# Attention with a softmax off by one and a gated long convolution: products of the shared keys with the values in tiles of 64 by 64

## The chip, the core and the metric

The kernel runs on one core of a Trainium2 chip, in one launch. The metric is the time of that launch on the device in microseconds (us). TensorE does the matrix products, VectorE (DVE), ScalarE (ACT) and GpSimd (POOL) do what is elementwise, SyncE (SP) issues most transfers.

## The reference, cut to what matters

```python
batch, n_heads, seq, head_dim = (8, 12, 448, 64)

def _attn_ref(q, k, v):
    scale = 1.0 / np.sqrt(q.shape[-1])
    scores = scale * np.matmul(q, k.transpose(0, 1, 3, 2))
    m = np.max(scores, axis=-1, keepdims=True)
    e = np.exp(scores - m)
    attn = e / (np.sum(e, axis=-1, keepdims=True) + np.exp(-m) + 1e-09)
    return np.matmul(attn, v).astype(np.float32)

def _moe_ref(x, w_proj, filter_fft, w_out):
    B, S, D = x.shape
    proj = x @ w_proj
    x1, x2, x3 = (proj[..., :D].copy(), proj[..., D:2 * D].copy(), proj[..., 2 * D:].copy())
    X2 = np.fft.rfft(x2, n=S, axis=1)
    H = np.fft.rfft(filter_fft, n=S, axis=0)[None, :, :]
    x2_conv = np.fft.irfft(X2 * H, n=S, axis=1)
    y = x1 * x2_conv * x3
    return (y @ w_out).astype(np.float32)
```

The output of attention, its heads side by side, is the `x` of the second function.

## The kernel before, in words

**Attention works on pairs of heads.** Eight batch elements of twelve heads make 48 pairs; `attention(i)` does pair `i`. A head has 448 keys: three tiles of 128 and a rest of 64. The rests of both heads of a pair share one tile (t = 0): rows 0 to 63 belong to head u = 0, rows 64 to 127 to head u = 1. These are the shared keys.

**Scores.** For the key tiles t = 1, 2, 3 `scores(t)` (L844) makes the transposed scores, keys on the partitions and queries along the free side, in quarters of the array: a head has 64 channels, so the two heads take the two halves of its rows, and the 128 keys of a tile are cut in two halves of 64 columns. Four matmuls (u and d) make one tile for both heads. The shared tile (L846) is one matmul of the full array. ScalarE takes the exponent (`exps`, L857 for t = 1, 2, 3 and L863 for the shared tile) into the bfloat16 tiles `e` and `er`.

**Value products.** Here the exponents are the stationary operand and the values (64 columns and a column of ones that gives the sum of the row, 65 in all) the moving one. Queries go in four tiles n of 128, the last of them padded. `out_rests` (L875) does the shared keys of both heads: for each n and each head u a matmul with 64 rows of `er` and 128 query columns, into the PSUM bank of that head. `out_rest(u)` (L883) adds the three full key tiles, twelve matmuls of the full array for each head. `norm` then divides on VectorE (L896 to L898).

**Where `out_rests` stands.** The program is written by a planner (`Plan`): every task names its engine, what it needs, makes, takes and gives, and a fixed list, `ORDER`, says in which order the tasks of each engine stand. Nothing is reordered at run time. `out_rests` of pair j is no task of its own in most cases; it is emitted at the end of a score task of the next pair, right behind the matmuls of L844:

```python
host = (2 if b == 0 or i % 2 == 0 else 3) if i and i != NHP else None
...
ex = with_rests(i - 1) if t == host else dict(cost=0.0, emit=lambda: None, ...)
```

Only at pairs 5 and 47 it is a task by itself. So 46 of the 48 stand behind L844.

**The second part.** `dense(b)` makes the three projections (L1072, L1094, L1194), the convolution by a short Fourier transform as matmuls (L1144, L1148, L1240), the gate on VectorE (L1209, L1284), and the output product (L1008), copied to SBUF by L1316 and sent out. Its tasks stand on TensorE between those of attention.

**Inputs.** q, k and v come in by transfers that SP issues; POOL casts them to bfloat16; from the third batch element on (`loaded`) the transposed keys and queries, `kT` and `qT`, are made by transposing transfers (L610, L603), and the output of attention is transposed in the same way into `xT` (L971).

Of the kernel before, what the change touches and what calls it, by code (L numbers as in the profile page):

```python
# [301 lines left out]
def kernel(  # L302
# [11 lines left out]
    nc = tc.nc  # L314
# [57 lines left out]
    vn = [const.tile([128, NHP, 7, DH + 1], BF16, name=f"vn{i}") for i in range(2)]  # L372
# [457 lines left out]
    def attention(i):  # L830
        b, hp = divmod(i, NHP)
        P = T.setdefault(i, {})
# [32 lines left out]
        def out_banks():  # L865
            return pair(("op", i))[:, :, 0 : NST * (DH + 1)].rearrange("p u (n d) -> p u n d", n=NST)

        def out_bank(u):
            return out_banks()[:, u]

        def out_rests():
            for n in range(NST):
                for u in range(2):
                    c = slice(64 * u, 64 * u + 64)
                    nc.tensor.matmul(  # L875
                        out_bank(u)[:, n, :], P["e"][0][c, n * 128 : n * 128 + 128], vn[b % 2][c, hp, 3, :],
                        start=(n == 0), stop=False,
                    )

        def out_rest(u):  # L880
            for n in range(NST):
# [65 lines left out]
        if i in (NHP - 1, n_batches * NHP - 1):  # L947
            ex = with_rests(i)
            add("PE", 0.19 + ex["cost"], tau(i, 1.1), out_rests, need=ex["need"], make=ex["make"], take=ex["take"],
                give=ex["give"])  # L950
# [650 lines left out]
```

## Time and profile before

| What | Value |
|---|---|
| timed runs | 381.67, 377.94, 381.98 us; median 381.67 us |
| the profiled execution | 380.34 us, span 378.6 us |
| TensorE busy | 366.5 us, 97% of the span, 3893 matmuls |
| ACT / DVE / POOL busy | 262.5 / 259.6 / 109.0 us |
| granted TensorE clock | 1.0 |
| transfers | 68.43 MB, mean 181 GB/s |

The profile is of one execution; the span goes from its first to its last instruction. A row of a timeline gives the start and length of a run of equal instructions in us, the engine, the line of the kernel, the operation, output and inputs, the tile of the array (rows * columns), the shapes, and how many there are. Matmuls are pipelined: one that lasts 0.19 us can be followed by the next after 0.03 us, so what a group takes from TensorE is read from its start to the start of what follows, not from its length. PEld are the loads of the stationary operand. In the views by windows there stand, for each stretch, its length, the busy time of the engines with the number of instructions in brackets, the granted clock, the share of busy time of the 16 DMA engines and GB/s; asked for one line, they count the instructions of that line that are in flight in the stretch. In the views of waits there stand, for each line and what it waited for, the total us, the times and the longest.

### The profile page before, as it was taken

How to read it: one execution, taken by the hardware profiler on the slowest of the kernel's cores; microseconds unless marked ns; L12 is line 12 of the kernel's file. 1: busy time of each engine (PE TensorE's matmuls, PEld its weight loads, DVE VectorE, ACT ScalarE, POOL GpSimd, SP SyncE). 2: the span in 40 equal slices, each digit the busy share in tenths (PEclk: the TensorE clock that was granted, in tenths of full speed). 3: DMA queues.
4: the chain of work that ended last, by engine and by line, in shares of the span. 5: the costliest groups of instructions: out<-in, count | busy, mean ns of one | idle time of the engine just before them, and what ended most of it. 6: DMA issues, size and time to landing. Idle time of an engine off the chain costs nothing. (4 is left out here: it accounts for less than half of the span.)

```text
span 378.6 us, 9895 instructions
## 1 busy us (share of the span) xinstructions
PE 366.5 (97%) x3893; PEld 216.8 (57%) x3893; DVE 259.6 (69%) x676; ACT 262.5 (69%) x455; POOL 109.0 (29%) x240
## 2 busy tenths in 40 slices
PE   8989999999999999998998999999999999999994
PEld 7666675556655665654565555565555555555552
DVE  7578587945898467594785777684386765758770
ACT  5878976776866777775686567877787866534533
POOL 4845536043441564124134430431120000000000
PEclk9999999999999999999999999999999999999999
DMA  8999999999999999974998999597965064035125
GB/s 220 272 251 231 240 250 170 146 196 225 232 214 260 245 212 246 207 180 107 234 216 226 271 213 238 179 212 164 198 131 121 2 85 113 15 85 126 44 87 167
DMA packets 132451, 68.43 MB, mean 181 GB/s; under 512 B 88813, under 2 KB 129200, under 8 KB 132400
## 3 DMA queue, kind: packets, MB, share of 16 engines
q1 hardware_dynamic: 127680, 62.11, 74.7%
q0 software_dynamic: 4480, 5.41, 8.8%
q8 instruction: 31, 0.51, 0.6%
q10 hardware_dynamic: 240, 0.23, 0.2%
q14 instruction: 20, 0.16, 0.1%
HBM read 43.86 MB, written 11.01 MB: 145 GB/s over the span
## 5 line engine op out<-in xcount | busy, mean ns | idle before, releaser
L857 ACT ACTIVATE e<-psum 128x896 bf16<-128x896 f32 x144 | 127.6, 924 | 25.9 <-PE psum L844 22.3
L1194 PE MATMUL psum<-xT,wproj_bf 128*128 128x448 bf16 x576 | 122.1, 352 | 0.2 <-DMA xT<-xb 0.2
L1194 PEld LDWEIGHTS <-wproj_bf 128*128 128x128 bf16 x576 | 54.1, 98 | 47.5 <-issue 3.8
L1008 PE MATMUL psum<-wout_bf,yT 128*128 128x384 bf16 x288 | 54.0, 326 | 0.2 <-DVE yT L1284 0.2
L883 PE MATMUL psum<-vn,e 128*128 128x65 bf16 x1152 | 46.8, 194 | 0.0
L1162 DVE TENSOR_TENSOR t<-xs,hrs 112x768 bf16<-112x768 bf16 (+1 forms) x64 | 36.9, 606 | 10.8 <-ACT xs L1156 10.8
L883 PEld LDWEIGHTS <-e 128*128 128x128 bf16 x1152 | 41.3, 98 | 5.0 <-issue 0.6
L844 PE MATMUL psum<-qT,kT 64*64 64x448 bf16 x576 | 43.1, 363 | 0.8 <-DMA kT<-nat 0.4
L1094 PE MATMUL psum<-xf,wproj_bf 128*128 128x452 bf16 x180 | 38.7, 356 | 1.2 <-DVE xf L1049 1.2
L1209 DVE TENSOR_TENSOR g<-x,psum 128x448 bf16<-128x448 bf16 x48 | 29.4, 618 | 13.6 <-PE psum L1194 8.6
L1008 PEld LDWEIGHTS <-yT 128*128 128x128 bf16 x288 | 27.2, 98 | 19.0 <-DVE yT L1284 1.1
L1156 ACT CAST xs<-psum 113x384 bf16<-113x384 f32 (+1 forms) x64 | 29.3, 488 | 11.8 <-PE psum L1144 9.5
L1206 ACT CAST x<-psum 128x448 bf16<-128x448 f32 x48 | 25.6, 536 | 16.5 <-PE psum L1194 15.7
L1316 ACT COPY osb<-psum 128x384 f32<-128x384 f32 x54 | 24.7, 492 | 16.2 <-SPq L1549 5.9
L863 ACT ACTIVATE er<-psum 128x448 bf16<-128x448 f32 x48 | 26.7, 555 | 13.2 <-PE psum L846 13.1
L639 POOL CAST nat<-nat 112x512 bf16<-112x512 f32 x36 | 22.9, 643 | 41.4 <-DMA nat<-in_q_dram 29.7
L898 DVE TENSOR_TENSOR xb<-psum,den 128x512 bf16<-128x512 f32 x48 | 33.2, 691 | 1.7
L671 POOL CAST vn<-nat 128x192 bf16<-128x192 f32 x58 | 21.6, 403 | 40.7 <-DMA nat<-in_v_dram 35.1
L896 DVE TENSOR_SCALAR den<-psum 128x8 f32<-128x8 f32 x48 | 7.8, 163 | 36.1 <-PE psum L883 34.7
L1249 ACT CAST cr<-psum 128x452 bf16<-128x452 f32 x48 | 24.4, 547 | 8.6 <-PE psum L1240 6.7
L1094 PEld LDWEIGHTS <-wproj_bf 128*128 128x128 bf16 x180 | 16.4, 96 | 18.0 <-issue 2.9
L1072 PE MATMUL psum<-wproj_bf,xf 128*113 128x384 bf16 x144 | 26.4, 327 | 0.0
(129 smaller groups left out, 465.2 us busy)
## 6 DMA issues: line engine op xcount, KB each, us to landing
nat<-in_q_dram SPq DMA_DIRECT2D x47, 224.0 KB, 4.4
out_dram<-osb SPq DMA_DIRECT2D x21, 384.0 KB, 3.5
nat<-in_k_dram SPq DMA_DIRECT2D x41, 192.0 KB, 4.4
nat<-in_v_dram SPq DMA_DIRECT2D x41, 192.0 KB, 4.4
wproj_bf<-in_moe_w_proj_dram POOLq DMA_DIRECT2D x2, 1152.0 KB, 14.0
out_dram<-osb SPq DMA_DIRECT2D x12, 192.0 KB, 3.1
rests<-in_k_dram SPq DMA_DIRECT2D x8, 192.0 KB, 4.7
rests<-in_v_dram SPq DMA_DIRECT2D x8, 192.0 KB, 4.5
```

Of the source, the lines that this page charges most:

```text
L844: nc.tensor.matmul(sc[r, u, 0:S], kT[b % 2][c, hp, t, r], qT[b % 2][c, hp, :])
L857: nc.scalar.activation(to, of, AF.Exp, scale=SCALE)
L863: nc.scalar.activation(to, of, AF.Exp, scale=SCALE)
L883: nc.tensor.matmul(out_bank(u)[:, n, :], P["e"][1 + t][:, u * S + n * 128 : u * S + n * 128 + 128], vn[b % 2][:, hp, 4 * u + t, :], start= ...
L898: nc.vector.tensor_tensor(W["xb", b][:, hp].rearrange("p n (u d) -> p u n d", u=2), op[:, :, :, 0:DH], rec[:].unsqueeze(3).to_broadcast([1 ...
L1008: nc.tensor.matmul(ops[:n, :DCH], y[:, dt, 0:n], wout_bf[:, dt, ch * DCH : (ch + 1) * DCH], start=(dt == 0), stop=(dt == NDT - 1),)
L1072: nc.tensor.matmul(pps[:FQ, :DCH], W["xf", b][:, pg, kt, 0:FQ], wproj_bf[:, kt, D + ch * DCH : D + (ch + 1) * DCH], start=(kt == 0), stop= ...
L1094: nc.tensor.matmul(pps, wproj_bf[:, kt, D + dt * 128 : D + (dt + 1) * 128], W["xf", b][:, :, kt, 0:FQ], start=(kt == 0), stop=(kt == NDT - 1),
L1156: nc.scalar.copy(L["xs", par, ch][:K, pg % 2, :], L["Z", pg, ch][:K, :DCH])
L1162: nc.vector.tensor_tensor(t[:K], L["xs", par, ch][:K], h, op=ALU.mult)
L1194: nc.tensor.matmul(p[:, :S], wproj_bf[:, kt, 2 * part * D + dt * 128 : 2 * part * D + (dt + 1) * 128], xT()[:, kt, 0:S], start=(kt == 0), ...
L1209: nc.vector.tensor_tensor(g[:, dt, :], L["x1", dt], p[:, :S], op=ALU.mult)
```

## The change

`out_rests` cuts the 128 query columns of each matmul into two halves of 64. Each half writes its own 64 partitions of the same PSUM bank. One group has sixteen matmuls then, in tiles of 64 rows by 64 columns, with sixteen weight loads; before it had eight in tiles of 64 by 128.

```diff
             for n in range(NST):
                 for u in range(2):
                     c = slice(64 * u, 64 * u + 64)
-                    nc.tensor.matmul(
-                        out_bank(u)[:, n, :], P["e"][0][c, n * 128 : n * 128 + 128], vn[b % 2][c, hp, 3, :],
-                        start=(n == 0), stop=False,
-                    )
+                    for d in range(2):
+                        o = n * 128 + 64 * d
+                        nc.tensor.matmul(
+                            out_bank(u)[64 * d : 64 * d + 64, n, :], P["e"][0][c, o : o + 64], vn[b % 2][c, hp, 3, :],
+                            start=(n == 0), stop=False,
+                        )
```

The order of all other instructions on every engine is the same in both kernels.

## The prediction

> **What bounds the kernel now.** I read first the head of the page: the span, the engines' busy time, the slices, then the chain that ended last.
>
> ```profile
> span 378.6 us, 9895 instructions
> PE 366.5 (97%) x3893; PEld 216.8 (57%) x3893; DVE 259.6 (69%) x676; ACT 262.5 (69%) x455; POOL 109.0 (29%) x240
> PEclk9999999999999999999999999999999999999999
> DMA  8999999999999999974998999597965064035125
> ```
>
> TensorE is busy for 97% of the span at the full granted clock, every other engine for 69% or less. But the 16 DMA engines also stand at nine tenths in most slices of the first half, so there a faster TensorE may find its inputs late. The chain of waits on the page covers only the last 5 us (output products of L1008) and says nothing of attention, so I read the waits of TensorE by stretch, in two answers, 0 to 73 us and 73 to 330 us.
>
> ```profile
> PE psum L980 <- DVE xb L898: 1.0, 2, 0.6
> ...
> PE psum L1094 <- DVE xf L1049: 1.2, 1, 1.2
> PE psum L846 <- ACT e L857: 1.0, 1, 1.0
> PE psum L844 <- DMA kT<-nat: 0.4, 1, 0.4
> PE psum L1008 <- DVE yT L1284: 0.2, 1, 0.2
> PE psum L1194 <- DMA xT<-xb: 0.2, 1, 0.2
> ```
>
> TensorE waits seldom, but these few places matter: time saved ahead of one is kept only if the producer named there also moves earlier. Next, the windows view, which shows where no such place exists (columns: length, then PE, PEld, DVE, ACT, POOL busy).
>
> ```profile
> 30.00:73.00 43.00, 42.65 (x495) 26.83 (x491) 34.76 (x92) 33.81 (x59) 18.97 (x38) 1.00 1.18 213
> ...
> 203.00:317.00 114.00, 114.00 (x1243) 62.67 (x1242) 75.11 (x202) 85.15 (x143) 20.31 (x44) 1.00 0.77 169
> ```
>
> From 203 to 317 us TensorE is busy for 114.00 of 114.00 us, and the DMA share has fallen to 0.77: there every nanosecond taken off TensorE should come off the span.
>
> **What the changed lines cost now.** The view of L875 gives 384 matmuls, eight for each of 48 pairs of heads. The timeline of TensorE shows one such group among its neighbours.
>
> ```profile
> L875 PE MATMUL psum<-vn,er x384: 187/192/202, 11.6 to 317.0; 64*128 64x65 bf16 x192
> ...
> 151.56 0.37 PE L1240 MATMUL psum<-bt,yh 113*128 113x113 bf16 x4
> 151.86 0.57 PE L844 MATMUL psum<-qT,kT 64*64 64x448 bf16 x8
> 152.36 0.30 PE L875 MATMUL psum<-vn,er 64*128 64x65 bf16 x8
> 152.59 0.38 PE L1240 MATMUL psum<-bt,yh 113*128 113x113 bf16 x4
> 152.81 0.54 PE L883 MATMUL psum<-vn,e 128*128 128x65 bf16 x12
> 153.19 1.14 PE L1008 MATMUL psum<-wout_bf,yR 128*128 128x384 bf16 x6
> ```
>
> A row's length includes the tail of its last matmul; what a group takes from TensorE is the distance from its start to the next start. Twelve L883 take 0.38 us, 32 ns each, and are followed by L1008 with no gap; four L1240 at 152.59 take 0.22 us, 55 ns each, and then comes L883. Both are changes of line among full-array matmuls, and neither costs anything visible. The four L1240 at 151.56, though, which are followed by L844 in tiles of 64 by 64, take 0.30 us: 0.08 more. The same loss stands between L844 and L875, and behind L875. To see it there I go down to the windows of L844 and L875 alone, in another pair of heads (columns: PE, then PEld), and the timeline at the seam.
>
> ```profile
> 157.50:157.56 0.06, 0.04 (x4) 0.04 (x7) 1.00 1.29 294
> 157.56:157.72 0.16, 0.16 (x4) 0.11 (x8) 1.00 1.30 296
> 157.72:157.80 0.08, 0.08 (x8) 0.00 (x0) 1.00 1.22 278
> ...
> 158.02:158.05 0.03, 0.02 (x2) 0.03 (x4) 1.00 1.24 410
> 158.05:158.09 0.04, 0.04 (x4) 0.04 (x6) 1.00 1.07 365
> 158.09:158.12 0.03, 0.03 (x6) 0.03 (x8) 1.00 0.97 333
> 158.12:158.15 0.03, 0.03 (x8) 0.03 (x7) 1.00 1.20 410
> ...
> 157.74 0.36 PE L844 MATMUL psum<-qT,kT 64*64 64x448 bf16 x4
> 158.03 0.20 PE L875 MATMUL psum<-vn,er 64*128 64x65 bf16 x1
> ...
> 158.03 0.29 PE L875 MATMUL psum<-vn,er 64*128 64x65 bf16 x8
> 158.26 0.93 PE L883 MATMUL psum<-vn,e 128*128 128x65 bf16 x24
> ```
>
> L844 runs in rounds of four: four in flight from 157.52, eight from 157.74. L875 runs in rounds of two: two, four, six, eight in flight, a new round about every 0.03 us, since the first is over after 0.20 us and all four after 0.29. So the number of rounds is what counts, not the number of matmuls. The second round of L844 ends at 157.74 + 0.36 = 158.10 us; the first round of L875 ends at 158.03 + 0.20 = 158.23, 0.13 us later, where a round of 65 columns needs 0.03. About 0.10 us is lost at the change from tiles of 64 by 64 to tiles of 64 by 128. Behind L875, 0.23 us pass until L883 for four rounds of 0.03: another 0.11.
>
> **The change part by part.** Each group gets 16 matmuls and 16 weight loads instead of eight and eight, in tiles of the shape that L844 has.
>
> Rounds: for each n there were two matmuls (u), now there are four (u and d), in four different quarters of the array, as in L844. Four rounds before, four after, of 65 columns each. Cost 0 if the four start together; four starts instead of two cost a few ns once, at the end of the group, and I take 6 ns from the step between starts that L844's first window bounds: four starts within 0.04 us, so 10 ns at most for each step.
>
> Seam ahead: 46 of the 48 groups are emitted inside a score task right behind L844 (`with_rests`); the two at the end of the first and the last batch element stand alone behind full-array matmuls and win nothing. For the 46 the shape no longer changes: 0.10 us is removed. Less the 6 ns: 0.095 us a group, 46 × 0.095 = 4.4 us of TensorE.
>
> Seam behind: tiles of 64 by 64 to full array instead of 64 by 128 to full array. No row shows that it differs; L1240 to L844 loses 0.08 to 0.09 and L875 to L883 0.11, so I keep 0.11, change 0.
>
> Weight loads: the loads of L875 and of L844 stand thus.
>
> ```profile
> L875 PEld LDWEIGHTS <-er x384: 92/94/98, 11.6 to 317.0; 64*128 64x128 bf16 x192
> L844 PEld LDWEIGHTS <-kT x576: 102/103/107, 7.7 to 314.1; 64*64 64x64 bf16 x192
> L844 PE MATMUL psum<-qT,kT x576: 346/373/374, 7.7 to 314.3; 64*64 64x448 bf16 x192
> L761 PEld LDWEIGHTS <-sb x4: 128/134/134, 10.8 to 10.9; 113*113 113x113 bf16 x4
> L761 PE MATMUL psum<-ident_bf,sb x4: 217/217/260, 10.8 to 11.0; 113*113 113x113 bf16 x4
> ```
>
> A load of 64 columns takes 103 ns against 94, though it is half as wide. What of it would show if it weren't hidden is the difference between L844's slowest and fastest matmul, 374 − 346 = 28 ns (first and second round). Lower bound 0: the load of a round runs under the 0.03 us of the round before it, as in L761, where 113 columns are loaded behind matmuls of 113 columns and all but the first keep 217 ns. Upper bound 28 ns in each of the three later rounds, 84 ns a group, which leaves 0.01 us of the gain. I take 0, since L761 is the nearest row with a load as long as its matmul.
>
> The Trainium skill speaks against this: "TensorEngine Tiling (Array Packing)", under Gotcha 2, says that column tiling excludes the fast weight load, and "TensorE: Matmul & The Clock Gate", under LDWEIGHTS, puts a load at its columns over 1.2 a ns, 53 ns for 64. By that a round would be paced by the load at 53 instead of 31 ns, three times 22 ns a group, and an estimate from those pages leaves 0.03 us a group, 1.4 us in all. L844's 28 ns of exposed load is half of that figure.
>
> Waits and queues: the order on every engine stays, only TensorE's list gets 384 matmuls and 384 loads longer. The last matmul alone signals, as before; DVE, ACT, POOL and DMAs do the same work.
>
> **How much of 4.4 us arrives.** The windows of L875 count the groups by stretch (eight matmuls each), and the timeline shows the wait at 73 us and the issue of the transfer behind it.
>
> ```profile
> 0.00:73.00 73.00, 3.26 (x88) 1.94 (x88) 1.00 1.13 227
> 73.00:203.00 130.00, 5.62 (x152) 3.44 (x152) 1.00 1.00 210
> 203.00:317.00 114.00, 5.10 (x140) 3.07 (x142) 1.00 0.77 169
> ...
> 60.42 1.20 SPq L610 DMA_TRANSPOSE kT<-nat  x1
> 73.00 0.57 PE L844 MATMUL psum<-qT,kT 64*64 64x448 bf16 x8 [0.36 <-DMA kT<-nat]
> ```
>
> That makes 11, 19 and 18 groups, of which 10, 19 and 17 follow L844. The transposed keys for 73 us were issued 12.6 us earlier, with the DMA share at 1.18; loads, casts and transfers set this landing, not TensorE. So the 10 × 0.095 = 0.95 us saved before it turn into a longer wait there: kept 0. Between 73 and 203 us, 19 × 0.095 = 1.8 us are saved, and four waits of 0.2, 1.2, 1.0 and 0.2 us stand in the way, each on an engine or transfer that itself follows TensorE's results at some distance; bounds 0 and 1.8. I take 60%, 1.1 us, since three of the four are on DVE and ACT, which get earlier input too. From 203 us on, 17 × 0.095 = 1.6 us, kept whole. Sum 2.7 to 2.9; I take 2.8. The profiled execution took 380.34 us, 1.7 over its span: 380.34 − 2.8 = 377.5 us. The timed runs of before (377.94 to 381.98, median 381.67) lie around 380.34, so against that median the result could read 1.3 higher; the range allows for it. About 1% is what a measurement of this kernel can tell from no change.
>
> **The rivals.** *All of it arrives:* the waits before 203 us give way because loads are freed earlier too. 46 × 0.095 = 4.4: 376.0 us. For it: 97% busy; against it: the transfer issued 12.6 us ahead and the DMA share over 1.
>
> *None of it arrives:* waits eat it, or the 28 ns of load show in each round. 380.3 us. For it: the first half is as full on DMA as on TensorE; against: 114.00 busy of 114.00 from 203 us on.
>
> *The column halves run after each other:* two matmuls in flight stay the limit at short streams, so a group has eight rounds of 31 ns: 4 × 31 = 124 ns more, less 100, times 48: +1.2 us, 381.5. For it: no row has four short matmuls together; against: L844's rounds of four.
>
> *One at a time, the slower side:* if the pace is set for each matmul, as in L883 (0.38 us for 12, 32 ns), 16 take 0.51 us instead of 0.12, so 0.39 − 0.10 = 0.29 us more a group, times 48: +14 us, 394. It decides from 14 ns a matmul on: 16 × 14 = 0.22 us is what four rounds (0.12) and the seam (0.10) take now. Against it: L875 now starts two in each 0.03 us. The Trainium skill's "TensorE: Matmul & The Clock Gate", under the question of 56 and 53.3 ns, has such a floor, about 25 ns from start to start however short the stream; here pairs start closer than that, so it does not hold between tiles.
>
> **How the numbers follow.** Forecast 0.55, all 0.17, none 0.12, halves 0.09, one at a time 0.07. Faster by over 1% means a gain above 3.8 us: all of it, most of 0.17, and the forecast's upper end, 0.12: 0.28. Slower by over 1%: one at a time 0.07 and a little of the halves: 0.09. The rest, 0.63, is within 1%. The range runs from 374.5 (all of it, with the spread of runs) to 382 (halves).
>
> **What would show it.** Right: in the timeline L844 ×8 to L875 falls from 0.50 to 0.40 us, L875 lists 768 matmuls in rounds of four with 0.23 us until L883, its load near 103 ns; TensorE's busy time falls by some 4 us, and the wait on the transposed keys near 73 us grows from 0.4 to over 1 us. Wrong: L875 to L883 takes 0.31 us or more (loads or halves), or 0.6 (one at a time), or the seam ahead stays at 0.13.

## The result, and the profile after

Over 13 runs each, the changed kernel takes 376.89 us (375.46 to 378.98) and the kernel before 380.29 us (377.94 to 383.32). The ratio is 0.991, 95% interval 0.9881 to 0.9939: 3.4 us less, between 2.3 and 4.5. The profiled execution took 377.19 us. In the profile after, the head of the page and the busy time of TensorE read thus.

```profile
span 375.4 us, 10663 instructions
PE 361.7 (96%) x4277; PEld 221.4 (59%) x4277; DVE 259.7 (69%) x676; ACT 262.7 (70%) x455; POOL 111.8 (30%) x240
```

TensorE has 384 matmuls more and is busy for 4.8 us less; the busy time of DVE and ACT is the same within 0.2 us. The forecast was 377.5 us. The lines behind the change have moved by two: L883 is L885, L1194 is L1196, L1240 is L1242, and L875 is now L877. The timeline of TensorE after the change, at the two pairs of heads that the prediction showed:

```profile
151.27 0.37 PE L1242 MATMUL psum<-bt,yh 113*128 113x113 bf16 x4
151.56 0.57 PE L844 MATMUL psum<-qT,kT 64*64 64x448 bf16 x8
151.97 0.30 PE L877 MATMUL psum<-vn,er 64*64 64x65 bf16 x16
152.20 0.38 PE L1242 MATMUL psum<-bt,yh 113*128 113x113 bf16 x4
...
157.13 0.57 PE L844 MATMUL psum<-qT,kT 64*64 64x448 bf16 x8
157.53 0.29 PE L877 MATMUL psum<-vn,er 64*64 64x65 bf16 x16
157.76 0.93 PE L885 MATMUL psum<-vn,e 128*128 128x65 bf16 x24
```

From L844 to the shared keys it is 0.40 to 0.41 us (before 0.50 to 0.51), and from there to what follows 0.23, as before. Sixteen matmuls take what eight took. The windows of L877 show why (columns: length, then PE and PEld of that line), and the view of the line gives the durations.

```profile
157.52:157.55 0.03, 0.02 (x4) 0.01 (x4) 1.00 1.11 358
157.55:157.58 0.03, 0.03 (x8) 0.03 (x8) 1.00 1.05 358
157.58:157.61 0.03, 0.03 (x12) 0.03 (x12) 1.00 0.90 307
157.61:157.64 0.03, 0.03 (x16) 0.03 (x12) 1.00 1.20 410
...
L877 PEld LDWEIGHTS <-er x768: 102/107/111, 12.1 to 313.6; 64*64 64x64 bf16 x192
L877 PE MATMUL psum<-vn,er x768: 187/192/215, 12.3 to 313.6; 64*64 64x65 bf16 x192
```

Four, eight, twelve, sixteen in flight: four rounds of 0.03 us, as before with two each. The loads got longer (107 against 94 ns), yet the matmuls' median stays at 192 ns and the rounds at 0.03 us: behind L844 the loads are hidden.

Where the time arrives is read from the same landmarks in both timelines: the score task at 73 us (before, then after), and the last group of shared keys with what follows it (before, then after).

```profile
73.00 0.57 PE L844 MATMUL psum<-qT,kT 64*64 64x448 bf16 x8 [0.36 <-DMA kT<-nat]
73.70 0.57 PE L844 MATMUL psum<-qT,kT 64*64 64x448 bf16 x8
...
316.93 0.29 PE L875 MATMUL psum<-vn,er 64*128 64x65 bf16 x8
317.16 0.33 PE L883 MATMUL psum<-vn,e 128*128 128x65 bf16 x5
...
313.47 0.32 PE L877 MATMUL psum<-vn,er 64*64 64x65 bf16 x16
313.72 0.93 PE L885 MATMUL psum<-vn,e 128*128 128x65 bf16 x24
```

In this pair of executions the changed kernel reaches the 73 us task 0.70 us later and the last group 3.46 us earlier. All of the gain of this pair comes from behind the first, and 36 groups of 0.10 are 3.6 of the 4.2 us between the two landmarks. A second execution of the changed kernel has the landmarks at 73.60 and 314.29 us, 3.2 us closer together than before. The place of the first landmark alone says little: it moves by up to 2.9 us between executions that don't differ ahead of it (see the last experiment).

The last group stands behind a full-array product and not behind L844. It takes 0.25 us until L885, where it took 0.23 before. Probably the loads of its first round show here, which have no round of the same shape to hide under (the slowest matmul of L877 takes 215 ns, the median 192); the change loses a little in the two groups that stand so.

The waits of TensorE after the change say what held the beginning (0 to 73.6 us), and what was left behind it (73.6 to 200 us):

```profile
PE psum L1074 <- DMA wproj_bf<-in_moe_w_proj_dram: 1.0, 1, 1.0
PE psum L846 <- DVE xT L991: 1.0, 1, 1.0
PE psum L535 <- POOL ldm L494: 0.9, 2, 0.8
...
PE psum L1242 <- DVE g L1211: 0.4, 1, 0.4
PE psum L1010 <- DVE yT L1286: 0.4, 1, 0.4
PE psum L846 <- DMA qT<-nat: 0.4, 1, 0.4
```

Before 73.6 us TensorE now waits for weights, for POOL's cast of keys and for a copy on DVE, places where it did not wait or waited less before. Between the two landmarks the waits sum to 2.6 us before and 2.2 after: the one for DVE's `xf` of 1.2 us near 172 us is gone in this execution, but others have come. The 0.4 us of difference are most of what exceeds the 36 groups. In the second execution the wait for `xf` is there again, with 1.1 us.

### The profile page after: what moved, and what is told of

It is laid out like the page before. It is cut to its first block, busy times and chain, and to the rows that moved or that the text cites. A ratio compares the mean times of both kernels' runs of the same rounds, so it can differ in the third digit from the quotient of the medians.

```text
span 375.4 us, 10663 instructions
## 1 busy us (share of the span) xinstructions
PE 361.7 (96%) x4277; PEld 221.4 (59%) x4277; DVE 259.7 (69%) x676; ACT 262.7 (70%) x455; POOL 111.8 (30%) x240
## 5 line engine op out<-in xcount | busy, mean ns | idle before, releaser
L1196 PE MATMUL psum<-xT,wproj_bf 128*128 128x448 bf16 x576 | 121.9, 352 | 0.2 <-DVE ldm L1107 0.2
L1196 PEld LDWEIGHTS <-wproj_bf 128*128 128x128 bf16 x576 | 54.1, 98 | 47.4 <-issue 3.8
L885 PE MATMUL psum<-vn,e 128*128 128x65 bf16 x1152 | 46.7, 194 | 0.0
L885 PEld LDWEIGHTS <-e 128*128 128x128 bf16 x1152 | 41.3, 97 | 4.5 <-issue 0.6
L844 PE MATMUL psum<-qT,kT 64*64 64x448 bf16 x576 | 42.8, 362 | 0.4 <-ACT e L857 0.3
L639 POOL CAST nat<-nat 112x512 bf16<-112x512 f32 x36 | 24.3, 684 | 45.7 <-DMA nat<-in_q_dram 32.3
```

What stands on the lines that cost most here:

```text
L844: nc.tensor.matmul(sc[r, u, 0:S], kT[b % 2][c, hp, t, r], qT[b % 2][c, hp, :])
L885: nc.tensor.matmul(out_bank(u)[:, n, :], P["e"][1 + t][:, u * S + n * 128 : u * S + n * 128 + 128], vn[b % 2][:, hp, 4 * u + t, :], start= ...
L1196: nc.tensor.matmul(p[:, :S], wproj_bf[:, kt, 2 * part * D + dt * 128 : 2 * part * D + (dt + 1) * 128], xT()[:, kt, 0:S], start=(kt == 0), ...
```

## Experiments

**The seam moved instead of removed.** Half of the query tiles in the new shape, half in the old:

```diff
 for n in range(NST):
+    w = 64 if n < 2 else 128
...
-        for d in range(2):
+        for d in range(0, 128, w):
...
```

> Query tiles n = 0 and 1 in tiles of 64 by 64, n = 2 and 3 in tiles of 64 by 128: half of the change's matmuls, but the change of shape between L844 and the full array isn't removed, only moved into the middle of the group. Theory (the seam is what the change saves): the time of before within 0.5%, about 380 us; the seam behind L844 near 0.02 us, a new one of about 0.10 us in the group. Rival (tiles of 64 by 64 are in themselves quicker): half of the gain, about 378.5 us.

Measured: 381.0 us against 380.17, ratio 1.0036 (1.0006 to 1.0065). The timeline:

```profile
156.70 0.36 PE L844 MATMUL psum<-qT,kT 64*64 64x448 bf16 x4
156.89 0.40 PE L878 MATMUL psum<-vn,er 64*64 64x65 bf16 x12
157.22 0.92 PE L886 MATMUL psum<-vn,e 128*128 128x65 bf16 x24
```

The group follows L844's round after 0.19 us, without a seam, but takes 0.33 us until L886 instead of 0.23. What was taken away in front stands in the middle, and the gain is gone. The new shape by itself wins nothing; what wins is that the shape doesn't change.

**More seams.** The same with n = 0 and 2 in 64 by 64, 1 and 3 in 64 by 128:

```diff
-    w = 64 if n < 2 else 128
+    w = 64 if n % 2 == 0 else 128
```

> The same with n = 0 and 2 in 64 by 64 and n = 1 and 3 in 64 by 128: three changes of shape inside a group, two more than in the kernel before counted with the seams around it. Theory: 0.10 us for each, 48 x 2 x 0.10 = 9.6 us more than before, about 390 us. Rival (the seam costs because of what follows, not because of the shape): no more than 1 us above before.

Measured: 388.92 us, ratio 1.0234 (1.0184 to 1.0285), 8.9 us more (7.0 to 10.8).

```profile
161.96 0.57 PE L844 MATMUL psum<-qT,kT 64*64 64x448 bf16 x8
162.36 0.63 PE L878 MATMUL psum<-vn,er 64*64 64x65 bf16 x12
162.92 0.27 PE L886 MATMUL psum<-vn,e 128*128 128x65 bf16 x3
```

The group now takes 0.56 us: 0.33 more for three changes of shape inside it, 0.11 each. The price of a change holds with two more of them.

**The same agreement the other way round.** The kernel before, with the scores brought to the shape of the value products:

```diff
-                    for d in range(2):
-                        r = slice(64 * d, 64 * d + 64)
-                        nc.tensor.matmul(sc[r, u, 0:S], kT[b % 2][c, hp, t, r], qT[b % 2][c, hp, :])
+                    nc.tensor.matmul(sc[:, u, 0:S], kT[b % 2][c, hp, t, :], qT[b % 2][c, hp, :])
```

> The kernel before with the scores of the full key tiles in tiles of 64 by 128 (two matmuls a key tile instead of four) and the shared keys as before, in 64 by 128: the shapes at the seam agree the other way round. Theory: the seam behind L844 goes as well, 46 x 0.10 = 4.7 us of TensorE, and at the way into L844 the narrower load no longer shows (28 ns in L844's first round now, about 13 at the load of 128 columns), some 80 times 0.01 = 1 us more; 375.5 to 377.5 us. Rival (what counts is the 64 by 64 form of the value products): the time of before, 380 us.

Measured: 376.18 us, ratio 0.9905 (0.9867 to 0.9943).

```profile
161.54 0.55 PE L842 MATMUL psum<-qT,kT 64*128 64x448 bf16 x4
161.93 0.28 PE L873 MATMUL psum<-vn,er 64*128 64x65 bf16 x8
162.15 0.36 PE L844 MATMUL psum<-qT,kT 128*128 128x448 bf16 x1
```

From the scores to the shared keys 0.39 us, and 0.22 to the next: the seam is gone although the value products are untouched. With the two runs before it, this settles the cause. Both ways were then run beside each other.

> The changed kernel once more, beside the next run on the same chip: about 377 us, 0.991 of before.

> The kernel with scores in 64 by 128 and the shared keys left in 64 by 128, beside the changed kernel. Theory (both take away the same seam; the load of 64 columns that shows at the way into L844 is some 10 to 15 ns longer, about 80 times): 0.5 to 1 us less than the changed kernel, 376 to 376.5 us. Rival: no difference, 377 us.

Measured: the changed kernel 377.92 us, ratio 0.9909 (0.9872 to 0.9946); scores in 64 by 128 377.08 us, ratio 0.9882 (0.9851 to 0.9912). The intervals overlap; the expected 0.5 to 1 us between them is neither shown nor excluded.

**Halves one after the other.** The loop over d moved outside:

```diff
+for d in range(2):
     for n in range(NST):
         for u in range(2):
-            for d in range(2):
```

> The changed kernel with the column halves one after the other: all d = 0 first, then all d = 1, so that two quarters at a time can work together, eight rounds instead of four. Theory (the count of rounds sets the time of a group): 4 x 0.031 = 0.12 us more a group than in the changed kernel, 48 x 0.12 = 6 us of TensorE, 382 to 383 us. Rival (the order doesn't matter, the array takes what is free): the time of the changed kernel, 377 us.

Measured: 378.55 us, ratio 0.9949 (0.9914 to 0.9984). My theory missed; the rival was nearer.

```profile
158.98 0.33 PE L877 MATMUL psum<-vn,er 64*64 64x65 bf16 x16
159.24 0.93 PE L885 MATMUL psum<-vn,e 128*128 128x65 bf16 x24
```

0.26 us instead of 0.23: one round more, not four. Matmuls of the second half must have begun while earlier ones of the first half still waited for their quarters. To see how far this goes, the loops were turned quarter by quarter:

```diff
+for u in range(2):
+    for d in range(2):
+        for n in range(NST):
-for n in range(NST):
-    for u in range(2):
-        for d in range(2):
```

> The changed kernel with the sixteen matmuls of a group quarter by quarter: four n in one quarter of the array, then four in the next. Theory from the run with the halves (a quarter takes its next matmul as soon as it is free, past matmuls that wait for another quarter): little more than the four rounds plus the time to get past the others, some 0.15 to 0.2 us between first and last start, 0.27 to 0.32 us until what follows; 378 to 381 us. Rival (matmuls start in the program's order): the next quarter starts only with the last n of the one before, 13 rounds, 0.37 us between first and last start, 0.27 us more a group than in the changed kernel, 48 x 0.27 = 13 us of TensorE, 387 to 390 us.

Measured: 378.8 us, ratio 0.9951 (0.9928 to 0.9975). The timeline, and the windows of L877:

```profile
158.41 0.34 PE L877 MATMUL psum<-vn,er 64*64 64x65 bf16 x16
158.69 0.92 PE L885 MATMUL psum<-vn,e 128*128 128x65 bf16 x24
...
158.40:158.43 0.03, 0.01 (x2) 0.01 (x2) 1.00 2.73 384
158.43:158.46 0.03, 0.03 (x5) 0.03 (x6) 1.00 0.97 333
158.46:158.49 0.03, 0.03 (x8) 0.03 (x10) 1.00 0.82 282
158.49:158.52 0.03, 0.03 (x11) 0.03 (x13) 1.00 0.97 333
158.52:158.55 0.03, 0.03 (x14) 0.03 (x15) 1.00 0.82 282
158.55:158.58 0.03, 0.03 (x16) 0.03 (x11) 1.00 0.75 256
```

Two are in flight by the first window, then some three more in each 0.03 us. Four in one quarter, one after another at 0.03 us a round, would make one in each 0.03 us and 0.37 us between the first and the last start; here all sixteen started within 0.17. The group takes 0.28 us, 0.05 more than in the changed order.

**Where saved time arrives.** In the kernel before, the shared keys were left out of the value products in one stretch of pairs at a time: 0 to 10, 11 to 29, or 30 to 47.

```diff
+gone = 11 <= i < 30
 def out_rests():
-    for n in range(NST):
+    for n in range(0 if gone else NST):
...
-                        start=False,
+                        start=gone and n == 0 and t == 0,
```

> The kernel before, with the shared keys left out of the value products in the first 11 pairs (up to about 73 us): 11 x 0.23 us = 2.5 us of TensorE less, all of it ahead of the wait on the transposed keys. Theory (that landing is set by loads, casts and transfers): 0 to 0.8 us less than before. Rival (time saved early arrives as well as late): 2.5 us less, 377.7 us.

> The same left out in the next 19 pairs (73 to 203 us): 19 x 0.23 = 4.4 us of TensorE less. Theory (60% arrives): 2.6 us less than before. Rivals: all, 4.4; none, 0.

> The same left out in the last 18 pairs (203 to 317 us, where TensorE never waits): 18 x 0.23 = 4.1 us of TensorE less. Theory: 3.9 to 4.1 us less than before. Rival (another engine or the transfers are as late as TensorE there): half or less, 2 us.

| Stretch | TensorE time left out | ratio (95%) | arrived |
|---|---|---|---|
| to 73 us | 2.5 us | 1.0018 (0.9983 to 1.0053) | none (0.6 less to 2.0 more) |
| 73 to 203 us | 4.4 us | 0.9952 (0.9921 to 0.9982) | 1.8 us (0.7 to 3.0) |
| 203 to 317 us | 4.1 us | 0.9866 (0.9836 to 0.9897) | 5.1 us (3.9 to 6.2) |

The timeline of the first of these at the 73 us task, and then the same task in the two others, whose instructions up to it are those of the kernel before:

```profile
71.78 0.54 PE L1196 MATMUL psum<-xT,wproj_bf 128*128 128x448 bf16 x2
74.39 0.57 PE L844 MATMUL psum<-qT,kT 64*64 64x448 bf16 x8 [2.07 <-DMA kT<-nat]
...
74.17 0.57 PE L844 MATMUL psum<-qT,kT 64*64 64x448 bf16 x8 [0.74 <-DMA kT<-nat]
75.91 0.57 PE L844 MATMUL psum<-qT,kT 64*64 64x448 bf16 x8 [1.12 <-DMA kT<-nat]
```

The wait for the transposed keys is 2.07 us here, and 0.36, 0.74 and 1.12 us in the three executions with an unchanged first stretch. All waits of TensorE up to this task sum to 7.7 us, against 3.4, 5.0 and 6.0; besides the keys, the waits for DVE's `xb` have grown (2.2 us against 1.0 to 1.4). The time that TensorE saved early stands in such waits. One execution each can't give its size; the ratio in the table does. In the late stretch more arrived than was left out; its interval reaches down to 3.9 us, so it shows that nearly all or all of the 4.1 us arrives, and the rest has no cause shown.

## Why the prediction was right, point by point

*The seam.* Forecast 0.10 us for each of 46 groups; measured 0.09 and 0.11 at the two places above. The mixed, the alternating and the turned-round kernels show that the change of shape is the cause. *Rounds:* four of 0.03 us before and after; both the halves and the one-at-a-time rivals are out for the changed kernel. *Loads:* taken as hidden, and hidden in the groups behind L844. The estimate from the Trainium skill's "TensorEngine Tiling (Array Packing)", under Gotcha 2, and "TensorE: Matmul & The Clock Gate", under LDWEIGHTS, 53 ns a round and a gain of 1.4 us on TensorE, is not what happened: rounds stay at 0.03 us. *Seam behind:* unchanged, the group takes 0.23 us from start to start as before. *TensorE busy:* 4.8 us less, where 4.4 was worked out. The 6 ns that were taken off for four starts in a round show in no row; without them 46 × 0.10 is 4.6.

*How much arrives.* This was the loosest term. Early: nothing, as taken. Middle: 60% taken, 40% in the run with the middle left out (16 to 68%), so probably too much. Late: whole, as taken (3.9 to 6.2 of 4.1 us). With these shares the sum is 0 + 0.4 × 1.8 + 1.6 = 2.3 us, at the lower edge of the measured 2.3 to 4.5. The forecast of 2.8 us lies inside; the other 0.6 up to the measured middle of 3.4 is within the uncertainty of the measurement and has no cause shown. That the forecast came as near as it did owes something to the 60%, a guess that lies above the 40% of the run with the middle left out: in part that was luck. That all of the saved time would arrive, 4.4 us, is not excluded by the interval of the result alone; it is by the early groups.

*A sign that failed.* The wait for the transposed keys near 73 us was to grow to over 1 us. In the profiled execution after the change it isn't there: TensorE waited for weights, POOL and DVE ahead of it. In the second run of the changed kernel it is there, with 1.1 us:

```profile
PE psum L844 <- DMA kT<-nat: 1.1, 1, 1.1
```

But the same line stands, with the same 1.1 us, in the run with the late stretch left out, where nothing ahead of 73 us differs from the kernel before; so this growth doesn't show that time was saved ahead of it. The early stretch is held by loads, casts and transfers together, and which of them is last differs from execution to execution. The step that said "nothing arrives early" rests on the run with the early stretch left out; one wait in one execution was too narrow a sign for it.

*The halves rival* supposed that two matmuls in flight stay the limit. They don't: a round of the changed kernel starts four. Its price of 124 ns a group was used again for the kernel with the halves written one after the other, and there 0.03 us was measured. The step of that expectation that failed is the premise that matmuls begin in the program's order.

## What to carry to other kernels

Count changes of tile shape on TensorE, not only matmuls: put products of one shape side by side, or bring a small one to its neighbour's shape, and each change that goes saves about 0.1 us. Ask then in which stretch the time is saved, because the same saving was worth nothing where transfers set the pace and its whole amount where TensorE never waited. Leaving out work in one stretch at a time measures that share directly, here to within about 1.2 us.

## What the runs showed of the hardware that was not expected

The list `ORDER` fixes the order in the program, but matmuls in different quarters of the array need not start in it: sixteen matmuls written quarter by quarter, four times four in a row, started within 0.17 us where one quarter after the other would need 0.37. A bad order still costs something, 0.28 against 0.23 us a group. A change of tile shape cost about 0.1 us in every direction seen: 0.09 to 0.11 us from 64 by 64 to 64 by 128, 0.11 for each of the three there and back in the alternating kernel, 0.11 from either of them to the full array (0.23 less four rounds of 0.03), and 0.08 from the full array to 64 by 64.
